# Attention and two feed-forward layers on one core: a shared block of tail keys, and fp32 value products in column halves of TensorE

## The chip, the cores and the metric

The kernel runs on one core of a Trainium2 chip. The metric is the device time of one execution in microseconds (us); lower is better. A difference of 0.2% (some 2.3 us here) is about the least that a measurement of this kernel tells from no change.

## The reference

Inputs are `q`, `k`, `v` of shape (4, 8, 576, 64) in fp32: 4 batches, 8 heads, 576 positions, 64 dimensions. Weights come in float64.

```python
q_rot, k_rot = (rotate(q), rotate(k))
scores = scale * np.matmul(q_rot, k_rot.transpose(0, 1, 3, 2))
scores = scores - np.max(scores, axis=-1, keepdims=True)
attn = np.exp(scores)
attn = attn / (np.sum(attn, axis=-1, keepdims=True) + 1e-09)
attn_out = np.matmul(attn, v).astype(np.float32)
x = attn_out.transpose(0, 2, 1, 3).reshape(B * S, H * D)   # 2304 x 512
h = x @ w_in;  g = h * np.clip(h + 3.0, 0.0, 6.0) / 6.0;  x = g @ w_out      # 512 -> 2048 -> 512
h = x @ w_in2; g = h / (1.0 + np.exp(-1.702 * h));        out = g @ w_out2
```

## The kernel before

A planner (`Plan`) collects operations with an engine, a duration, a sort key and their buffers; `run` simulates the engines with these durations and writes each engine's instructions in the order that it finds. The table `C` holds the keys' offsets and buffer counts (`PB`, `PTB`). So a change to an operation's cost or key reorders the program far from it.

**fp32 by pieces.** A fast product takes operands in the type fp32r, which keeps fewer bits. To reach fp32 accuracy, an operand is split into a high part (a copy in fp32r) and a low part (the difference): names that end in `h` and `l`. A product is then three fast products (`qh kh`, `ql kh`, `qh kl`). A plain fp32 product needs no split; on TensorE (PE) it is two matmul records in the trace.

**Attention** (`attention`, `pair`) goes by pairs of heads, 16 in all, 4 for each batch. For a pair:
- q and k are rotated (mostly on GpSimd, POOL), transposed on PE (L498, L511) and split. `vhl` is the split of the values `rawv`, 64 high and 64 low columns for each of the 10 blocks.
- Queries are blocks c = 0 to 3 of 128, and a block of the last 64 of either head (`P[8]`). `both` makes the scores of block c for both heads (L558): each head uses 64 rows of PE, so the two heads' products stand in the two row halves. `tail` makes those of the last queries (L545). VectorE (DVE) takes the maximum of each 576 keys (L531), ScalarE (ACT) the exponential (L533) into a buffer `P`.
- Values: for each head, the five key blocks j = 0 to 4 (the fifth has 64 keys) of `P` are transposed on PE, four transposes for a block (L611, 40 in a pair). ACT copies a block out of PSUM to `PTh` (L615), DVE takes the low part `PTl` (L632) or, for the tail block, puts it below the high part (L619). Then two products with `vhl` (L638), or one for the tail block (L623), give 128 rows: the part of the values' high columns and that of their low columns. In batches 0 and 1 some blocks j go as a plain fp32 product instead (L628): 64 columns of PE, `PTh` unsplit; the table's `F00` to `F21` say how many, 4 a pair in batch 0, 5 in batch 1, none in batches 2 and 3. ACT copies half of the bank to `otmp`, DVE adds (L645), and a product with the transposed reciprocal sums (L670, L678) finishes the pair.
- The last queries: `P[8]` is transposed (L580), split in `P8h` and `P8l`, and multiplied in nine products (L598); ACT and DVE join the two halves (L661, L663), and L672 transposes.

**The first layer** (`moe1`) runs batch by batch while the next batch's attention goes on, so its products (L814, L839) stand between the attention's; batch 0 has no layer beside it, only the weights' conversion (L719 to L728). The second layer (L1027 to L1139) follows when attention is done.

Of the kernel before, what the change touches and what calls it, by code (L numbers as in the profile page):

```python
# [30 lines left out]
C = {'T0': 59.504, 'D1': 12.604, 'LN1': 168.009, 'LN2': 130.306, 'LN3': 403.413, 'LM': 383.596, 'X': 32.498,  # L31
# [7 lines left out]
HOOK = None  # L39

# [40 lines left out]
class Plan:  # L81
# [70 lines left out]
    def run(self):  # L152
# [39 lines left out]
        def place(o):  # L192
# [16 lines left out]
            if at and sum(f) < 2 and nxt["PS"][0] not in o.news:  # L209
                return None  # L210
            return at

        def can(o):
# [6 lines left out]
            for t, k in need.items():  # L220
                room = self.caps[t] - used[t]
                if room < k:
                    return False
                if room <= k and any(b not in o.news for b in nxt[t][:k]):
                    return False
# [12 lines left out]
        total = len(self.ops)  # L238
        while done < total:
            moved = True  # L240
            while moved:
                moved = False
                for e in engines:
# [15 lines left out]
                    if e == "PE" and o.mode != mode:  # L259
                        for x in ready[e]:  # L260
                            if x.key[0] > o.key[0] + C["MODE"]:
                                break
                            if x.mode == mode and can(x):
                                o = x
                                break
                    for x in o.alts:
                        ready[x].remove(o)
                    o.ns, o.fn = o.alts[e]
                    for b, i in place(o):
# [10 lines left out]
                    if e == "PE":  # L280
                        if o.mode != mode:
                            o.ns += 95
                        mode = o.mode
# [11 lines left out]
                    for x in o.begun:  # L295
                        x.n -= 1
                        if x.n == 0:
                            x.taken = (now, o)
                            heapq.heappush(events, (max(now, x.t0), seq, "put", x))
                            seq += 1  # L300
            if not events:
# [43 lines left out]

def act(n, psum=False, acc=False):
    return (170 if psum else 205) + 0.833 * n + 200 * acc
# [19 lines left out]
def attention_moe_moe(ctx: ExitStack, tc: tile.TileContext, q, k, v, w_in, w_out, w_in2, w_out2,  # L367
# [49 lines left out]
    def full(b, n, h):  # L417

        return C[f"F{min(b, 2)}{h}"]

    def attention(apool, pp, gpool, wtile, tabs, xf_of, at):
# [5 lines left out]
        for i, (r, parts) in enumerate(((rq, ((64, 128, 0), (0, 64, 1))), (rk, ((64, 128, 0), (64, 128, 1))))):  # L427
            def zero(r=r, parts=parts):
                for lo, hi, h in parts:
                    nc.gpsimd.memset(r.t[lo:hi, h, 4, :], 0.0)  # L430
            plan.op("Pool", 200, -100 + i, zero, w=[(r, "z")])

        def pair(n):
# [19 lines left out]
            rv = Buf(plan, apool, "rawv", [128, 2, 5, D], F32, 2)  # L453
            sm = v[b, h0:h0 + 2, 0:512, :].rearrange("h (p r) d -> p h r d", r=4)
            tl = v[b, h0:h0 + 2, 512:576, :].rearrange("h p d -> p h d")
            kv = kd + 1.0
            plan.op("SP", 475, kv, lambda: nc.sync.dma_start(rv.t[:, :, 0:4, :], sm), w=[(rv, 0)], kb=256, after=[lq])
            plan.op("SP", 630, kv, lambda: nc.sync.dma_start(rv.t[0:64, :, 4, :], tl), w=[(rv, 1)], kb=64, after=[lq])
            plan.op("SP", 630, kv, lambda: nc.sync.dma_start(rv.t[64:128, :, 4, :], tl), w=[(rv, 2)], kb=64, after=[lq])
# [52 lines left out]
            kh = Buf(plan, apool, "kh", [128, S], F32R, 2)  # L512
            kl = Buf(plan, apool, "kl", [128, S], F32R, 2)
# [677 lines left out]
```

## Time and profile before

| | |
|---|---|
| time, median of 3 runs (lowest to highest) | 1135.84 us (1135.81 to 1136.01) |
| span of the profiled execution, first to last instruction | 1134.3 us, 1.5 us less than the median run |
| PE busy | 1098.7 us, 97% |
| DVE, ACT, POOL busy | 713.2, 558.9, 645.3 us |

No time of the profiled execution is given beside its span. PE is busy nearly all the time; how far its records overlap is read from the distance of their starts, since a record lasts longer than the distance to the next.

### The profile page before, as it was taken

How to read it: one execution, taken by the hardware profiler on the slowest of the kernel's cores; microseconds unless marked ns; L12 is line 12 of the kernel's file. 1: busy time of each engine (PE TensorE's matmuls, PEld its weight loads, DVE VectorE, ACT ScalarE, POOL GpSimd, SP SyncE). 2: the span in 40 equal slices, each digit the busy share in tenths (PEclk: the TensorE clock that was granted, in tenths of full speed). 3: DMA queues.
4: the chain of work that ended last, by engine and by line, in shares of the span. 5: the costliest groups of instructions: out<-in, count | busy, mean ns of one | idle time of the engine just before them, and what ended most of it. 6: DMA issues, size and time to landing. Idle time of an engine off the chain costs nothing.

```text
span 1134.3 us, 16742 instructions
## 1 busy us (share of the span) xinstructions
PE 1098.7 (97%) x6264; PEld 898.2 (79%) x6264; DVE 713.2 (63%) x1092; ACT 558.9 (49%) x1133; POOL 645.3 (57%) x640
## 2 busy tenths in 40 slices
PE   5999999999999999999999999999999999999995
PEld 4666777777888888878887888888888888888884
DVE  5788777877656665566664544655655655566543
ACT  5788766666755564655556412444323433333330
POOL 5875876969563477363326435466645647455440
PEclk9999999999999999999999999999999999999998
DMA  3434565656543545443337543122102011120012
GB/s 92 129 129 142 160 225 165 212 183 206 171 130 111 153 151 181 120 141 107 112 112 260 157 140 85 66 74 75 42 34 75 19 56 37 39 74 21 19 75 93
DMA packets 58888, 129.69 MB, mean 114 GB/s; under 512 B 13752, under 2 KB 26808, under 8 KB 58040
## 3 DMA queue, kind: packets, MB, share of 16 engines
q1 hardware_dynamic: 44712, 78.13, 21.4%
q0 software_dynamic: 13824, 50.34, 14.7%
q8 instruction: 49, 0.80, 0.3%
q14 instruction: 31, 0.25, 0.1%
q10 hardware_dynamic: 272, 0.16, 0.0%
HBM read 103.97 MB, written 24.64 MB: 113 GB/s over the span
## 4 chain that ended last, share of the span: by engine, by line
PE 92%; DVE 5%; ACT 1%; issue 0%; DMA 0%; SPq 0%; DVEq 0%; ACTq 0%
PE psum L839 17%; PE psum L1139 17%; PE psum L814 17%; PE psum L1027 11%; PE psum L1067 6%; PE psum L611 6%; PE psum L558 5%; PE psum L638 4%; PE psum L628 3%; PE psum L598 1%; PE psum L545 1%; DVE sc L531 1%; DVE cvt L728 1%; PE psum L498 1%; PE psum L580 1%; PE psum L623 1%
## 5 line engine op out<-in xcount | busy, mean ns | idle before, releaser
L391 POOL TENSOR_TENSOR gl<-t,gh 128x512 fp32r<-128x512 f32 (+1 forms) x144 | 184.4, 1284 | 138.0 <-ACT gh L401 118.9
L533 ACT ACTIVATE P<-psum,sc 128x576 f32<-128x576 f32 x144 | 105.5, 739 | 60.4 <-DVE sc L531 60.0
L531 DVE TENSOR_REDUCE sc<-psum 128x1 f32<-128x576 f32 x144 | 102.6, 752 | 35.4 <-PE psum L558 31.8
L1145 DVE TENSOR_TENSOR oacc<-oacc,psum 128x512 f32<-128x512 f32 x124 | 85.0, 686 | 48.9 <-PE psum L1139 47.4
L615 ACT ACTIVATE PTh<-psum 128x512 fp32r<-128x512 f32 (+2 forms) x160 | 89.0, 598 | 49.3 <-PE psum L611 48.0
L1139 PE MATMUL psum<-woh,gh 128*128 128x512 f32 x284 | 111.2, 392 | 0.0
L1139 PE MATMUL psum<-woh,gl 128*128 128x512 f32 x284 | 110.8, 390 | 0.0
L1139 PE MATMUL psum<-wol,gh 128*128 128x512 f32 x284 | 110.7, 390 | 0.0
L401 ACT ACTIVATE gh<-t 128x512 fp32r<-128x512 f32 (+1 forms) x134 | 81.1, 607 | 53.3 <-DVE t L1035 25.7
L814 PE MATMUL psum<-xh,wih 128*128 128x512 f32 x256 | 105.7, 413 | 1.5 <-DVE t L821 1.2
L839 PE MATMUL psum<-gh,woh 128*128 128x512 f32 x256 | 104.3, 407 | 0.1
L848 DVE TENSOR_TENSOR y<-y,psum 128x512 f32<-128x512 f32 x112 | 76.4, 685 | 42.5 <-PE psum L839 41.7
L814 PE MATMUL psum<-xh,wil 128*128 128x512 f32 x256 | 100.5, 393 | 0.0
L839 PE MATMUL psum<-gh,wol 128*128 128x512 f32 x256 | 100.4, 392 | 0.0
L814 PE MATMUL psum<-xl,wih 128*128 128x512 f32 x256 | 100.3, 392 | 0.0
L839 PE MATMUL psum<-gl,woh 128*128 128x512 f32 x256 | 100.2, 391 | 0.0
L821 DVE SCALAR_TENSOR_TENSOR t<-t,psum 128x512 f32<-128x512 f32 (+1 forms) x80 | 50.0, 631 | 68.2 <-ACT t L819 68.0
L611 PE MATMUL psum<-ident,P 128*128 128x128 f32 (+1 forms) x640 | 87.9, 275 | 2.7 <-ACT P L533 1.2
L611 PEld LDWEIGHTS psum<-ident,P 128*128 128x128 f32 (+1 forms) x640 | 71.6, 135 | 23.6 <-issue 4.7
L819 ACT ACTIVATE t<-psum,three 128x512 f32<-128x512 f32 (+1 forms) x80 | 50.7, 644 | 79.8 <-PE psum L814 62.4
L1035 DVE TENSOR_TENSOR t<-t,psum 128x512 f32<-128x512 f32 (+1 forms) x52 | 31.5, 606 | 78.3 <-ACT t L1033 68.1
L632 DVE TENSOR_TENSOR PTl<-psum,PTh 128x512 fp32r<-128x512 f32 x92 | 61.5, 685 | 29.0 <-ACT PTh L615 28.7
(193 smaller groups left out, 2936.7 us busy)
## 6 DMA issues: line engine op xcount, KB each, us to landing
raw<-in_moe_w_in_dram SPq DMA_DIRECT2D x32, 512.0 KB, 3.8
raw<-in_moe_w_out_dram SPq DMA_DIRECT2D x32, 512.0 KB, 3.6
wih<-w_hl POOLq DMA_DIRECT2D x24, 512.0 KB, 4.4
wil<-w_hl POOLq DMA_DIRECT2D x24, 512.0 KB, 5.2
woh<-w_hl POOLq DMA_DIRECT2D x24, 512.0 KB, 4.4
wol<-w_hl POOLq DMA_DIRECT2D x24, 512.0 KB, 5.0
rawq<-in_q_dram SPq DMA_DIRECT2D x16, 256.0 KB, 3.0
rawk<-in_k_dram SPq DMA_DIRECT2D x16, 256.0 KB, 2.8
```

The source lines that it names most:

```text
L391: alts = [("Pool", ns or gps(n), lambda: nc.gpsimd.tensor_tensor(o(), i0(), i1(), op=op)), ("DVE", dve(n), lambda: nc.vector.tensor_tensor ...
L401: alts = {"ACT": ("ACT", act(n, psum), lambda: nc.scalar.activation(o(), i(), AF.Copy, scale=scale)), "DVE": ("DVE", dve(n, not psum), lam ...
L531: plan.op("DVE", dve(S), key + C["oM"], lambda: nc.vector.tensor_reduce(sc.t[:, i:i + 1], Sp.t[:, :, :HS], axis=AX.XY, op=ALU.max, negate= ...
L533: plan.op("ACT", act(S, True, True), key + C["oE"], lambda: nc.scalar.activation(halves(P[i].t), Sp.t[:, :, :HS], AF.Exp, bias=sc.t[:, i:i ...
L611: nc.tensor.transpose(T.t[:m, 0, c * 128:c * 128 + 128], P[hs + c].t[:, j * 128:j * 128 + m], ident)
L615: plan.op("ACT", act(512, True), key + C["oTh"], lambda T=T, hi=hi, m=m, fp=fp: nc.scalar.activation(hi.t.bitcast(F32) if fp else hi.t[:m] ...
L814: nc.tensor.matmul(hp.t[:, 0, :n], ww.t[:, cc, fs], xx.t[:, cc, :n], start=(cc == 0 and i == 0), stop=(cc == CC - 1 and i == 2))
L839: nc.tensor.matmul(yp.t[:, 0, :n], ww.t[:, a, cs], xx.t[:, a, :n], start=(i == 0), stop=(i == 3 * G - 1))
L848: plan.op("DVE", dve(n), ka + C["oY"], lambda yp=yp, y=y, c=c, n=n: nc.vector.tensor_tensor(y.t[:, c, :n], y.t[:, c, :n], yp.t[:, 0, :n], ...
L1027: nc.tensor.matmul(hp.t[:, 0, :n], ww.t[:, cc, fs], xx.t[:, cc, :n], start=(cc == 0 and i == 0), stop=(cc == CC - 1 and i == 2))
L1139: nc.tensor.matmul(op_.t[:, 0], xx.t[:, ts], ww.t[:, a, :], start=(i == 0), stop=(i == 3 * G - 1))
L1145: plan.op("DVE", dve(512), key, lambda op_=op_, tt=tt: nc.vector.tensor_tensor(oacc.t[:, tt], oacc.t[:, tt], op_.t[:, 0], op=ALU.add), r=[ ...
```

## The change

All batches take one path now (`FP` lists all five blocks for each batch).
- The tail keys: `kh` and `kl` get 64 more columns in front, into which POOL copies the 64 tail keys. The second head's scores run over tail, then main keys, so that in the pair's joint buffer `P[c]` (1152 columns) the two heads' tails stand side by side. One transposed block of 128 keys serves both heads: 36 transposes for a pair. `rawv` holds the two heads' tail values in a block that is zero elsewhere (POOL clears it once).
- The values: no split. One fp32 product of the shared tail block over all 128 columns of PE, then for each j = 0 to 3 head 0's product into columns 0 to 63 and head 1's into columns 64 to 127, all in one bank and in one run. ACT copies the bank to `xf`; `otmp`, the addition, `vhl`, `PTl` and DVE's part in them are gone.
- The last queries: five fp32 products of 128 columns instead of nine split ones of 256.
- The planner's rules for banks and buffers, its costs for a change of PE's mode, and the table `C` are changed too.

```diff
+FP = ((0, 1, 2, 3, 4), (0, 1, 2, 3, 4), (0, 1, 2, 3, 4), (0, 1, 2, 3, 4))
...
+            for x in range(2):
+                plan.op("SP", 550, kv, lambda x=x: nc.sync.dma_start(
+                    rv.t[64 * x:64 * x + 64, 8 + x, :], v[b, h0 + x, 512:576, :]), w=[(rv, 1 + x)], kb=32, after=[lq])
...
+            for kk in (kh, kl):
+                plan.op("Pool", gps(64, True), key, lambda kk=kk: nc.gpsimd.tensor_scalar(
+                    kk.t[:, :64], kk.t[:, S:].bitcast(F32), 1.0, 1.0, op0=ALU.mult, op1=ALU.mult), r=[(kk, "m")], w=[(kk, "t")])
...
-                P[c], P[4 + c] = [Buf(plan, pp, "P", [128, S], F32, C["PB"]) for _ in range(2)]
+                P[c] = Buf(plan, pp, "P", [128, 2 * S], F32, C["PB"])
...
-                                                 kk.t[xs, hf * HS:(hf + 1) * HS], start=i == 0, stop=i == 2)
+                                                 kk.t[xs, 64 * (1 - x) + hf * HS:64 * (1 - x) + (hf + 1) * HS], start=i == 0, stop=i == 2)
...
+                    nc.tensor.matmul(E.t[:, 0, 128:256].rearrange("p (h d) -> p h d", h=2), h8.t[:, j * 128:j * 128 + 128],
+                                     rv.t[:, 0:8].rearrange("p (h j) d -> p h j d", h=2)[:, :, j] if j < 4 else rv.t[:, 8:10],
+                                     start=(j == 0), stop=(j == 4))
...
+                    off = 128 * j if j == 4 or h == 0 else S + 64 + 128 * j
...
+                            nc.tensor.transpose(T.t[:, 0, c * 128:c * 128 + 128], P[c].t[:, off:off + 128], ident)
...
+                        if j == 4 and allfp:
+                            nc.tensor.matmul(Os[0].t[:, 0], flat(rv.t[:, 8:10]), parts[4, 0][0].t.bitcast(F32), start=j == js[0], stop=False)
...
+                    for j in js:
+                        if j in fp and j < 4:
+                            for h in range(2):
+                                nc.tensor.matmul(Os[h].t[hrow(h), 0], rv.t[:, 4 * h + j], parts[j, h][0].t.bitcast(F32), start=False, stop=allfp and j == 3)
...
+            if allfp:
+                copy(key, 512, lambda: xf.t[:, hp, :512], lambda: Os[0].t[:, 0], [Os[0]], [(xf, h0), (xf, h0 + 1)], also=("ACT", "DVE"), psum=True)
```

How the order moves is shown at three places. The first is PE in batch 0, where the second pair's values are made. Before (transposes L611, a fast product L623, fp32 products L628):

```order
L611 MATMUL psum<-ident,P 128x128 x4
L628 MATMUL psum<-PTh,rawv 64x512
L611 MATMUL psum<-ident,P 128x128 x4
L628 MATMUL psum<-PTh,rawv 64x512
L611 MATMUL psum<-ident,P 128x128 x4
L611 MATMUL psum<-ident,P 64x128 x4
L623 MATMUL psum<-PTh,vhl 128x512
```

Now (L569 last queries' scores, L615 their products, L650 the tail block, L664 the column halves, L700 a transpose, L582 the next pair's scores):

```order
L569 MATMUL psum<-kl,qh 128x288
L615 MATMUL psum<-rawv,P8h 128x128 x5
L650 MATMUL psum<-PT,rawv 128x512
L664 MATMUL psum<-PT,rawv 64x512 x8
L700 MATMUL psum<-ident,t_622 128x128
L582 MATMUL psum<-kh,qh 128x288 x2
```

The fp32 products, one at a time between transposes before, stand in one run of eight behind the tail block. The second place is ACT, over the copies of a pair's transposed blocks in batch 0. Before (L615 the copies, L533 exponentials, L401 other copies, L515 `kh`):

```order
L515 ACTIVATE kh<-psum 128x576
L615 ACTIVATE PTh<-psum 128x512 x2
L401 ACTIVATE vhl<-rawv 128x10x64
L615 ACTIVATE PTh<-psum 128x512 x2
L401 ACTIVATE xh<-xf 128x512
L615 ACTIVATE PTh<-psum 64x512
L533 ACTIVATE P,sc<-psum,sc 128x576 x2
```

Now (L632 the copies, L557 exponentials, L535 `kh`, L424 other copies):

```order
L557 ACTIVATE P,sc<-psum,sc 128x576 x4
L535 ACTIVATE kh<-psum 128x576
L424 ACTIVATE P8h<-psum 128x512
L632 ACTIVATE PT<-psum 128x512 x9
L424 ACTIVATE P8h<-psum 64x128 x2
L557 ACTIVATE P,sc<-psum,sc 128x576 x2
```

All nine copies stand together, behind the pair's last exponentials and ahead of the next pair's first. The third place is PE in the last batch, where the first layer's products (L839; now L842) stand around a pair's values. Before:

```order
L598 MATMUL psum<-vhl,P8h 128x256
L638 MATMUL psum<-PTh,vhl 128x512
L638 MATMUL psum<-PTl,vhl 128x512
L839 MATMUL psum<-gh,woh 128x512
L839 MATMUL psum<-gl,woh 128x512
```

Now:

```order
L842 MATMUL psum<-xl,wih 128x512
L842 MATMUL psum<-xh,wil 128x512
L650 MATMUL psum<-PT,rawv 128x512
L664 MATMUL psum<-PT,rawv 64x512 x8
L582 MATMUL psum<-kh,qh 128x288 x2
```

The split products, spread in twos between the layer's, became one run here as well.

## Rows read from the trace of the kernel before

**Rows 1.** The page: busy time by engine, and the chain that ended last.

```profile
PE 1098.7 (97%) x6264; PEld 898.2 (79%) x6264; DVE 713.2 (63%) x1092; ACT 558.9 (49%) x1133; POOL 645.3 (57%) x640
...
PE 92%; DVE 5%; ACT 1%; issue 0%; DMA 0%; SPq 0%; DVEq 0%; ACTq 0%
```

**Rows 2.** Windows: stretch, length, then busy us of PE, PEld, DVE, ACT, POOL.

```profile
20.00:140.00 120.00, 111.70 (x733) 79.09 (x734) 96.73 (x144) 97.80 (x220) 92.33 (x84) 1.00 0.41 131
140.00:300.00 160.00, 159.29 (x896) 118.55 (x895) 119.95 (x179) 105.73 (x218) 123.09 (x113) 1.00 0.64 202
300.00:550.00 250.00, 250.00 (x1476) 204.23 (x1474) 157.01 (x245) 140.57 (x291) 133.81 (x146) 1.00 0.45 134
550.00:620.00 70.00, 67.76 (x389) 55.74 (x386) 45.24 (x69) 38.97 (x81) 27.49 (x31) 1.00 0.52 174
```

**Rows 3.** Chain that ended last, 40 to 75 us: start, us, what.

```profile
53.12 0.69 DVE PTh L619
...
53.86 0.73 PE psum L638 x2
```

**Rows 4.** Timeline of PE: start, us, line, out<-in, count, idle before.

```profile
32.47 1.93 PE L628 MATMUL psum<-PTh,rawv 128*64 128x512 f32 x4
...
47.23 0.71 PE L511 MATMUL psum<-ident,roped 128*128 128x128 f32 x5
47.77 1.91 PE L611 MATMUL psum<-ident,P 128*128 128x128 f32 x16
...
60.55 0.47 PE L623 MATMUL psum<-PTh,vhl 128*128 128x512 f32 x1
60.95 0.40 PE L558 MATMUL psum<-kh,qh 64*128 64x288 f32 x2
61.19 0.29 PE L558 MATMUL psum<-kh,ql 64*128 64x288 f32 x2
61.32 0.29 PE L558 MATMUL psum<-kl,qh 64*128 64x288 f32 x2
...
61.94 0.50 PE L638 MATMUL psum<-PTh,vhl 128*128 128x512 f32 x1
62.28 0.40 PE L638 MATMUL psum<-PTl,vhl 128*128 128x512 f32 x1
62.61 1.07 PE L628 MATMUL psum<-PTh,rawv 128*64 128x512 f32 x2
63.61 0.66 PE L580 MATMUL psum<-ident,P 128*128 128x128 f32 x4
...
64.68 0.40 PE L638 MATMUL psum<-PTh,vhl 128*128 128x512 f32 x1
64.92 0.39 PE L638 MATMUL psum<-PTl,vhl 128*128 128x512 f32 x1
...
67.24 0.28 PE L598 MATMUL psum<-vhl,P8h 128*128 128x256 f32 x1
67.36 0.29 PE L598 MATMUL psum<-vhl,P8l 128*128 128x256 f32 x1
...
69.74 0.71 PE L511 MATMUL psum<-ident,roped 128*128 128x128 f32 x5
```

**Rows 5.** Line L628: weight loads and records, ns minimum/median/maximum.

```profile
L628 PEld LDWEIGHTS psum<-PTh,rawv x72: 132/136/137, 29.5 to 273.3; 128*64 128x64 f32 x72
L628 PE MATMUL psum<-PTh,rawv x72: 592/592/644, 29.5 to 273.7; 128*64 128x512 f32 x72
```

**Rows 6.** Timeline of ACT: exponentials, then copies of transposed blocks.

```profile
24.52 0.73 ACT L533 ACTIVATE P<-psum,sc 128x576 f32<-128x576 f32 x1
...
25.24 0.74 ACT L533 ACTIVATE P<-psum,sc 128x576 f32<-128x576 f32 x1
...
25.96 2.07 ACT L615 ACTIVATE PTh<-psum 128x512 fp32r<-128x512 f32 x4
```

**Rows 7.** POOL groups by form: count, busy, mean ns, idle before.

```profile
L391 POOL TENSOR_TENSOR t<-rawk,tab 128x640 f32<-128x640 f32 x30 | 48.7, 1643 | 0.5
```

More of the change, by code (lines that the diff above doesn't have):

```diff
@@ L208, in place, with head @@
                 at.append((b, c[0]))
-            if at and sum(f) < 2 and nxt["PS"][0] not in o.news:
+            if at and sum(f) < 2 and not loose and head() not in o.news:
                 return None
             return at
+        def head():
+            for b in nxt["PS"]:
+                if all(x.tag == "PS" or used[x.tag] < self.caps[x.tag] for x in b.first.news):
+                    return b
         def can(o):
@@ L223, in can @@
                     return False
-                if room <= k and any(b not in o.news for b in nxt[t][:k]):
+                if (room <= k or t in STRICT) and any(b not in o.news for b in nxt[t][:k]):
                     return False
@@ L262, in run @@
                                 break
-                            if x.mode == mode and can(x):
+                            if not switch(mode, x.mode) and can(x):
                                 o = x
                                 break
+                    got = place(o)
+                    loose = False
                     for x in o.alts:
@@ L268, in run @@
                     o.ns, o.fn = o.alts[e]
[L269 removed]
+                    for b, i in got:
                         b.b0 = i
@@ L300, in run @@
                             seq += 1
+            if not events and not loose:
+                loose = True
+                if VERBOSE:
+                    print('loose', now)
+                continue
             if not events:
@@ L594, in pv8 @@
+            for x in range(2):
+                copy(key + C["oTh"], 128, lambda x=x: h8.t[64 * x:64 * x + 64, 512:], lambda: E.t[:64, 0, :128], [(E, 0)], [(h8, 1 + x)],
+                     also=("ACT", "DVE"), psum=True)
             def pv8():
                 for j in range(5):
-                    rh = vhl.t.rearrange("p (h j) a d -> p h j (a d)", h=2)[:, :, j]
-                    for i, x in enumerate((h8, l8) if j < 4 else (h8,)):
-                        nc.tensor.matmul(E.t[:, 0, 128:384].rearrange("p (h x) -> p h x", h=2), x.t[:, j * 128:j * 128 + 128], rh,
-                                         start=(j == 0 and i == 0), stop=(j == 4))
@@ L607, in pair, with tp @@
+            Os = [Banks(plan, 1)] * 2 if allfp else [Banks(plan, 1) for _ in range(2)]
+            parts = {}
+            for j in range(5):
+                for h in range(2) if j < 4 else (0,):
+                    key = f(C["TT"] + C["TS"] * (2 * j + h if j < 4 else -1 if allfp else 8))
                     T = Banks(plan, 1)
-                    def tp(T=T, j=j, m=m, hs=hs):
+                    off = 128 * j if j == 4 or h == 0 else S + 64 + 128 * j
+                    def tp(T=T, off=off):
@@ new lines, in pair @@
+                    hi = Buf(plan, pp, "PT", [128, 512], F32R, C["PTB"])
+                    if j in fp:
+                        plan.op("ACT", act(512, True), key + C["oTh"], lambda T=T, hi=hi: nc.scalar.activation(
+                            hi.t.bitcast(F32), T.t[:, 0], AF.Copy), r=[T], w=[hi],
+                            alts=[("DVE", dve(512), lambda T=T, hi=hi: nc.vector.tensor_copy(hi.t.bitcast(F32), T.t[:, 0]))])
+                        parts[j, h] = (hi, None)
+                        continue
@@ L632, in pair @@
+                    lo = Buf(plan, pp, "PT", [128, 512], F32R, C["PTB"])
+                    plan.op("ACT", act(512, True), key + C["oTh"], lambda T=T, hi=hi: nc.scalar.activation(
+                        hi.t, T.t[:, 0], AF.Copy), r=[T], w=[hi, lo])
                     plan.op("DVE", dve(512), key + C["oTl"], lambda T=T, hi=hi, lo=lo: nc.vector.tensor_tensor(
                         lo.t, T.t[:, 0], hi.t.bitcast(F32), op=ALU.subtract), r=[T, hi], w=[lo])
[L635 to L638 removed]
@@ L639, in pair @@
[L639 to L647 removed]
+                    parts[j, h] = (hi, lo)
@@ new lines, in pair @@
+            key = f(C["PV"] + C["TS"] * 9.5)
+            if allfp:
+                copy(key, 512, lambda: xf.t[:, hp, :512], lambda: Os[0].t[:, 0], [Os[0]], [(xf, h0), (xf, h0 + 1)], also=("ACT", "DVE"), psum=True)
+            else:
+                tmp = Buf(plan, pp, "otmp", [128, 512], F32, 1)
+                for h in range(2):
+                    copy(key, 512, lambda h=h: tmp.t[hrow(h)], lambda h=h: Os[h].t[hrow(1 - h), 0], [Os[h]], [(tmp, h)], also=("ACT", "DVE"), psum=True)
+                    plan.op("DVE", dve(512), key, lambda h=h: nc.vector.tensor_tensor(
+                        xf.t[hrow(h), hp, :512], Os[h].t[hrow(h), 0], tmp.t[hrow(h)], op=ALU.add),
+                        r=[Os[h], (tmp, h)], w=[(xf, h0 + h)])
```

161 lines of the change are left out of this document (68 added, 93 removed), and 14 rows, old and new, of the table C.

## Prediction

> **What bounds the kernel now.** I read the page first: PE is busy 97% of the span and the chain that ended last is 92% PE [rows 1]. Then the windows, since an average hides stages. From 300 to 550 us PE has no idle time at all, from 140 to 300 us 0.7 us; only from 20 to 140 us, where batch 0's attention has no layer beside it, is it idle 8.3 us of 120, with DVE and ACT at 81% each [rows 2]. Another 2.2 us are lost from 550 to 620, where attention ends. So nearly everywhere the time is the sum of PE's own work, and relief of DVE, ACT and POOL is worth something only in batch 0. There the chain runs through DVE too: a tail block's low part, 0.69 us, ends just ahead of the two products that use it [rows 3]. That stage goes by pairs: the transposes of k (L511) start at 47.23 and 69.74, so a pair takes 22.51 us [rows 4].
>
> Busy time can't price PE's work, as records overlap; I take distances of starts [rows 4]. Twenty-one transposes against five: 16 in 1.91 us and 5 in 0.71, so 1.20 for 11, **0.109** each. A fast product of 512 columns: 64.68 to 64.92 and the next, **0.23**. One of 256: 67.24 to 67.36, **0.12**. An fp32 record in 64 columns: four take 1.93 us, the last runs 0.592 [rows 5], so (1.93 - 0.592) / 3 = **0.446**, two records a product. Two row halves together: 61.19 to 61.32, **0.13** for both. That equals what one such product would need alone, so two halves of PE do work at once in this kernel; it is shown for row halves of fast products only.
>
> **The change part by part.**
>
> *Transposes.* 36 a pair for 40: 64 x 0.109 = **-7.0 us**.
>
> *Value products.* Before, 216 fast products (8 x 4 x 2 less those in fp32, and the tail blocks: 92 x 2 + 32) x 0.23 = 49.7, and 36 fp32 products x 2 x 0.446 = 32.1; together 81.8. Now, a pair: the tail block over 128 columns, two records of 512 columns, 0.89 (the row is for 64 columns; the number of moving columns is the same). Then eight products in column halves. Nothing in the trace shows two column halves at once. If each had to wait for the other: 16 x 0.446 = 7.14. If all overlapped: 8 x 0.446 = 3.57. The order issues head 0's two records ahead of head 1's two; if records start in order and a half takes one at a time, head 1 runs one record behind and the run takes 9 x 0.446 = 4.01. I take 4.01: the row halves overlap fully, which is the nearest row, and in the single fp32 products the weight loads of 0.136 already hide behind the records (0.446 is the whole distance) [rows 4, 5]. 16 x (0.89 + 4.01) = 78.4: **-3.4 us**. By batches: it costs 0.8 us a pair where there were no fp32 products (batches 2 and 3) and gives back 0.9 and 1.4 in batches 0 and 1. Bounds: -10.5 to +46.7.
>
> The Trainium skill, "TensorE: Matmul & The Clock Gate", section "What overlaps and what doesn't", says that weight loads overlap running matmuls only where their rows of the array differ. Two column halves share all rows, so by that rule 16 loads of 0.136 a pair would lie open, 35 us in all; the single column half above, whose loads hide, does not agree with it.
>
> *Last queries.* 144 records x 0.12 = 17.3 before; now five fp32 products with 128 moving columns, ten records a pair. None of that shape is in the trace; nearest is the fp32 transpose, 128 columns, 0.109: 17.4, **+0.1**. Were it 0.23, +19.
>
> *Changes of PE's division.* Products in a column half cost time at both ends: 61.94 to 62.61 is 0.67 for two fast products (0.46 elsewhere), and 62.61 to 63.61 is 1.00 for 0.89 [rows 4]. That is 0.32; only the exit's 0.11 is seen everywhere; I take 0.25. The order has 30 such stretches before and 16 now: 14 x 0.25 = **-3.5** (bounds -1.5, -4.5). Row-half stretches go from 62 to 57; entry and exit of one cost 0.17 and 0.2 (60.55 to 60.95 for 0.23, then 0.99 to 61.94 for 6 x 0.13). Against these five stand a dozen more alternations of transposes with the layer's products; I take both together as nothing.
>
> *Other engines.* DVE loses 92 low parts, 32 tail parts, 32 additions and more, ACT the copies to `otmp` and `vhl`, POOL a few splits. Past 140 us these are hidden by PE, so nothing is gained. POOL gets two copies of 64 columns a pair, on which the second head's scores wait; behind it in POOL's queue stand rotations. They follow `kh` and `kl` while PE does 36 transposes, 3.9 us: no cost. If POOL is in the middle of a rotation, 1.64 us [rows 7], still none; if that cover were gone, at most some 2 us a pair in batch 0, +8. SP issues as many transfers as before, two of them of half the size.
>
> *Waits in batch 0.* PE's work in one of its pairs before: 60 transposes 6.5, scores 24 x 0.13 + 6 x 0.13 = 3.9, four fp32 products 3.6, ten fast ones 2.3, nine of 256 columns 1.1, changes of division about 2.2: 19.6. The pair took 22.5, so 2.9 was waiting. Now: 56 transposes 6.1, scores 3.9, values 4.9, last queries 1.1, changes 1.1: 17.1. Will PE wait as much? An exponential follows the one before at 25.24 - 24.52 = 0.72; copies follow at (2.07 - 0.6) / 3 = 0.49 [rows 6]; DVE's maxima keep the exponentials' pace. From the last exponential of a pair at 0: PE transposes until 3.9, ACT's nine copies end at 5.2 behind them; scores of block 0 and of the last queries, their product, the tail block and the column halves fill PE until 12.5 and need three exponentials, long done. Then the scores of blocks 1, 2, 3 come at once, six exponentials with little on PE between: block 2 waits about 1.1 us for PSUM, and the next 36 transposes about 1.2 us for the last exponential, at 19.4. So 2.3 of waiting for 2.9: 0.6 x 4 pairs, and little else: **-2.0**. Bounds: all 8.3 us of idle time gone, or the 22.5 us a pair kept, which gives 2.5 x 4 = 10 us of the sum back.
>
> **Sum.** -7.0 - 3.4 + 0.1 - 3.5 - 2.0 = -15.8. From the median of 1135.8 (the span of 1134.3 and 1.5 around it) that is **1120.0 us**.
>
> **Rivals.**
> 1. *Column halves do not overlap, slower than before.* Place: the run of eight. Price: 7.14 for 4.01, 3.13 x 16 = +50: 1170. It decides from a run longer than 4.01 + 15.8 / 16 = 5.0 us, an overlap factor under 7.14 / 5.0 = 1.43. For it: no row shows column halves at once. Both streams need all 128 rows, which row halves don't. Against it: row halves overlap wholly, and an fp32 record takes 0.446 for what a fast one does in 0.23, so each stream asks for columns at half the pace.
> 2. *They overlap in part.* With a factor of 1.6 the run takes 7.14 / 1.6 = 4.46, +0.45 x 16 = +7: 1127. The Trainium skill, same page, "Measured speedup vs the span model", gives 2.38 for three column tiles, which is 1.59 for two in proportion; no run here shows it.
> 3. *Batch 0 keeps its 22.5 us a pair*, because the exponentials of three blocks stand in a row: +10 for what PE saves there and the 2.0: 1130.
> 4. *Batch 0's waits vanish.* DVE loses the low parts that ended PE's waits [rows 3], and the planner fills the gaps: -6 more, 1114.
>
> **How the numbers follow.** The forecast, 1116 to 1124, 0.57. Rival 1: 0.08; rival 2: 0.13; rival 3: 0.07; rival 4 (1108 to 1116): 0.15. Rival 1 is the slower side, with half of that beyond 1160. The range leaves it out and the edge of rival 4: **1110 to 1130**. Faster 0.89, within 0.2% (2.3 us, the least that a measurement of this kernel tells from no change) 0.03, slower 0.08.
>
> **What would show it.** In the profile after: the column halves' run from L664's first start to the next line's, 4.0 to 4.2 us (1: 7; 2: 4.5); last queries' records 0.11 apart; the distance of k's transposes in batch 0, 19 to 20 us; PE idle between 20 and 140 us, 5 to 8 us; none from 150 to 550. DVE's busy time falls by more than 100 us with no gain past 140 us. The prediction is wrong if the run is over 5 us, if new waits appear on PE beside the first layer (values now need all nine copies at once), or if the second head's scores wait for POOL.

## The result, and the profile after

| | before | after |
|---|---|---|
| time, median (lowest to highest) | 1135.82 us (1135.80 to 1136.01) | 1120.44 us (1120.09 to 1120.67) |
| ratio, 95% interval | | 0.9864 (0.9850 to 0.9878) |
| span of the profiled execution | 1134.3 us | 1118.1 us |

The gain is 15.4 us of median and 16.2 us of span. The page of the changed kernel, as in [rows 1]:

```profile
PE 1076.9 (96%) x6216; PEld 870.8 (78%) x6216; DVE 588.4 (53%) x877; ACT 538.8 (48%) x1104; POOL 636.6 (57%) x668
...
PE 88%; ACT 3%; POOL 3%; DVE 2%; DMA 2%; issue 1%; SPq 0%; DVEq 0%; POOLq 0%; ACTq 0%
```

DVE is busy 125 us less, and PE's share of the chain fell from 92% to 88%: PE waits more than before. The windows tell where. These are the stretches of [rows 2]; behind the five engines' busy times stand the granted clock of TensorE, the DMA share and GB/s:

```profile
20.00:140.00 120.00, 107.29 (x744) 77.99 (x746) 70.19 (x99) 97.87 (x223) 90.45 (x95) 0.97 0.45 149
140.00:300.00 160.00, 156.04 (x925) 117.93 (x922) 92.92 (x131) 104.18 (x219) 119.67 (x118) 1.00 0.58 190
300.00:550.00 250.00, 250.00 (x1465) 191.44 (x1465) 102.78 (x152) 129.54 (x275) 130.97 (x154) 1.00 0.45 137
550.00:620.00 70.00, 68.86 (x392) 56.60 (x392) 33.17 (x47) 39.72 (x83) 31.20 (x35) 1.00 0.55 184
```

PE's idle time in these stretches is 12.7, 4.0, 0 and 1.1 us; in [rows 2] it was 8.3, 0.7, 0 and 2.2. That is 6.6 us more, 4.4 of it in batch 0. Over the whole span PE's busy time fell by 21.8 us and its idle time (the span less the busy time) rose by 5.6 us, from 35.6 to 41.2. The next view is PE's timeline in batch 0 (start, us, line, idle time before and its releaser):

```profile
24.44 0.74 PE L531 MATMUL psum<-ident,roped 128*128 128x128 f32 x5 [1.06 <-ACT P L557]
...
45.48 0.77 PE L531 MATMUL psum<-ident,roped 128*128 128x128 f32 x5 [0.34 <-ACT P L557]
...
53.79 1.28 PE L615 MATMUL psum<-rawv,P8h 128*128 128x128 f32 x10
54.90 1.02 PE L650 MATMUL psum<-PT,rawv 128*128 128x512 f32 x2
55.86 3.65 PE L664 MATMUL psum<-PT,rawv 128*64 128x512 f32 x16
59.44 0.33 PE L700 MATMUL psum<-ident,t 128*128 128x128 f32 x1
...
62.90 0.40 PE L582 MATMUL psum<-kh,qh 64*128 64x288 f32 x2 [1.56 <-ACT P L557]
...
66.47 0.77 PE L531 MATMUL psum<-ident,roped 128*128 128x128 f32 x5
...
85.53 0.40 PE L582 MATMUL psum<-kh,qh 64*128 64x288 f32 x2 [2.46 <-ACT P L557]
...
89.61 0.77 PE L531 MATMUL psum<-ident,roped 128*128 128x128 f32 x5
```

Four things are read here. The run of column halves lasts 59.44 - 55.86 = 3.58 us. Inside it the records start in twos, as these cuts of the same timeline show:

```profile
56.34 0.60 PE L664 MATMUL psum<-PT,rawv 128*64 128x512 f32 x2
56.77 0.60 PE L664 MATMUL psum<-PT,rawv 128*64 128x512 f32 x2
```

The second two start 0.48 us behind the first, each further two 0.43 behind the ones before, and the next line 0.53 behind the last. So the 16 records need eight steps, and the two halves work at once with nothing lost. A single column half has the same steps in the kernel before (cuts of the first row of [rows 4]):

```profile
32.95 0.59 PE L628 MATMUL psum<-PTh,rawv 128*64 128x512 f32 x1
33.38 0.59 PE L628 MATMUL psum<-PTh,rawv 128*64 128x512 f32 x1
```

The prediction's 0.446 is thus the mean of one step of 0.48 and two of 0.43; by the starts a run of n steps takes n x 0.43 and 0.15 for its first step and its end. The last queries' ten records take 54.90 - 53.79 = 1.11, 0.11 each. The transposes of k stand 21.04, 20.99 and 23.14 us apart. And PE waits 1.56 and 2.46 us in the middle of a pair's scores (L582) for an exponential (L557) that frees their bank in PSUM.

### The profile page after: what moved, and what is told of

Read it like the earlier page. It is cut to its first block, busy times and chain, and to the rows that moved or that the text cites. A ratio compares the mean times of both kernels' runs of the same rounds, so it can differ in the third digit from the quotient of the medians.

```text
span 1118.1 us, 16407 instructions
## 1 busy us (share of the span) xinstructions
PE 1076.9 (96%) x6216; PEld 870.8 (78%) x6216; DVE 588.4 (53%) x877; ACT 538.8 (48%) x1104; POOL 636.6 (57%) x668
## 4 chain that ended last, share of the span: by engine, by line
PE 88%; ACT 3%; POOL 3%; DVE 2%; DMA 2%; issue 1%; SPq 0%; DVEq 0%; POOLq 0%; ACTq 0%
PE psum L1167 17%; PE psum L842 17%; PE psum L867 17%; PE psum L1055 11%; PE psum L1095 6%; PE psum L582 5%; PE psum L664 4%; PE psum L628 4%; PE psum L615 1%; ACT P L557 1%; PE psum L650 1%; PE psum L569 1%; POOL t L414 1%; PE psum L518 1%; PE psum L698 1%
## 5 line engine op out<-in xcount | busy, mean ns | idle before, releaser
L555 DVE TENSOR_REDUCE sc<-psum 128x1 f32<-128x576 f32 x144 | 102.4, 751 | 96.7 <-PE psum L582 81.4
L557 ACT ACTIVATE P<-psum,sc 128x576 f32<-128x576 f32 x144 | 105.6, 739 | 61.2 <-DVE sc L555 60.3
L842 PE MATMUL psum<-xh,wih 128*128 128x512 f32 x256 | 109.2, 426 | 0.0
L424 ACT ACTIVATE gh<-t 128x512 fp32r<-128x512 f32 (+1 forms) x134 | 81.0, 605 | 44.6 <-DVE t L1063 24.7
L842 PE MATMUL psum<-xh,wil 128*128 128x512 f32 x256 | 100.3, 392 | 0.0
L842 PE MATMUL psum<-xl,wih 128*128 128x512 f32 x256 | 100.3, 392 | 0.0
L849 DVE SCALAR_TENSOR_TENSOR t<-t,psum 128x512 f32<-128x512 f32 (+1 forms) x80 | 50.2, 632 | 94.8 <-ACT t L847 94.8
L632 ACT ACTIVATE PT<-psum 128x512 f32<-128x512 f32 x144 | 79.7, 611 | 37.7 <-PE psum L628 37.6
L628 PE MATMUL psum<-ident,P 128*128 128x128 f32 x576 | 77.9, 273 | 3.0 <-ACT P L557 1.6
L628 PEld LDWEIGHTS psum<-ident,P 128*128 128x128 f32 x576 | 66.9, 141 | 14.5 <-ACT P L557 2.4
L1055 PE MATMUL psum<-yh,wih 128*128 128x512 f32 (+1 forms) x208 | 74.9, 360 | 0.0
```

Source lines behind the costliest of these rows:

```text
L424: alts = {"ACT": ("ACT", act(n, psum), lambda: nc.scalar.activation(o(), i(), AF.Copy, scale=scale)), "DVE": ("DVE", dve(n, not psum), lam ...
L555: plan.op("DVE", dve(S), key + C["oM"], lambda: nc.vector.tensor_reduce(sc.t[:, i:i + 1], Sp.t[:, :, :HS], axis=AX.XY, op=ALU.max, negate= ...
L557: plan.op("ACT", act(S, True, True), key + C["oE"], lambda: nc.scalar.activation(halves(to()), Sp.t[:, :, :HS], AF.Exp, bias=sc.t[:, i:i + ...
L628: nc.tensor.transpose(T.t[:, 0, c * 128:c * 128 + 128], P[c].t[:, off:off + 128], ident)
L632: plan.op("ACT", act(512, True), key + C["oTh"], lambda T=T, hi=hi: nc.scalar.activation(hi.t.bitcast(F32), T.t[:, 0], AF.Copy), r=[T], w= ...
L842: nc.tensor.matmul(hp.t[:, 0, :n], ww.t[:, cc, fs], xx.t[:, cc, :n], start=(cc == 0 and i == 0), stop=(cc == CC - 1 and i == 2))
```

## The experiments

**1. Do column halves overlap, and what sets the run?** The second head's products behind all of the first's:

```diff
-                    for j in js:
-                        if j in fp and j < 4:
-                            for h in range(2):
+                    for h in range(2):
+                        for j in js:
+                            if j in fp and j < 4:
```

> The changed kernel, with the run of eight column-half products in another order: head 0's four blocks, then head 1's four, instead of the heads by turns; nothing else moves. In the profile of the changed kernel the run takes 3.58 us, 8 x 0.447, and its records start in twos. Theory A, PE starts records in the order of the program and a half takes one at a time: now eight records of one half stand ahead of the other half's, so nothing overlaps, the run takes 16 x 0.446 = 7.1 us, and the time is 1120.4 + 16 x 3.55 = 1177 us, a little less where batch 0 waits anyhow. Theory B, PE fetches records of the free half from behind, or a half's record is short by itself: run 3.6 us, time 1120 us.

1145.21 us, ratio 1.0080 (1.006 to 1.010). PE's timeline, first of the run's beginning alone, then of the whole run; behind it windows of its three thirds (records of L664 in brackets; one that runs over a boundary counts on both sides):

```profile
57.55 1.93 PE L664 MATMUL psum<-PT,rawv 128*64 128x512 f32 x4
...
57.55 5.42 PE L664 MATMUL psum<-PT,rawv 128*64 128x512 f32 x16
62.90 0.33 PE L700 MATMUL psum<-ident,t 128*128 128x128 f32 x1
```

```profile
57.50:59.30 1.80, 1.75 (x4) 0.60 (x5) 1.00 0.00 0
59.30:61.10 1.80, 1.80 (x10) 0.73 (x9) 1.00 0.00 0
61.10:62.90 1.80, 1.80 (x6) 0.40 (x3) 1.00 0.00 0
```

The run is 62.90 - 57.55 = 5.35 us, not the expected value of either theory. It is 12 steps (12 x 0.43 + 0.15 = 5.31): four records of head 0 stand alone (1.93 us for four, as for single products in [rows 4]), then records come in twos, and at the end four of head 1 stand alone. The profile doesn't name a record's half, but strict order would need 15 steps. So a record for the free half starts ahead of records that still wait for the other half, but only some four places ahead: the ninth record starts with the fifth. In the kernel's own order, two records of each head by turns, the free half always finds one within reach. 1.77 us more in 16 runs would be 28.3 us; 24.8 was measured.

The same question from the other side: of j = 0 to 2, head 1's products go into the first half too and are added to head 0's, so that only the last product of head 1 is alone in its half.

```diff
-                                nc.tensor.matmul(Os[h].t[hrow(h), 0], rv.t[:, 4 * h + j], parts[j, h][0].t.bitcast(F32), start=False, stop=allfp and j == 3)
+                                nc.tensor.matmul(Os[h].t[hrow(h if j == 3 else 0), 0], rv.t[:, 4 * h + j], parts[j, h][0].t.bitcast(F32), start=False, stop=allfp and j == 3)
```

> The changed kernel, but for j = 0 to 2 both heads' products go into columns 0 to 63 (head 1's values are then added to head 0's, so the output is not the reference's); only j = 3 still has one head in each half. Order and number of instructions stay. If the short run comes from the two halves working at once, 12 records stand one after the other and 4 in twos: (12 + 2) x 0.446 = 6.2 us a run, +2.67 x 16 = +43, 1163 us. If a record of the fp32 product is simply short here (0.22 us), nothing changes: 1120 us.

1158.10 us, ratio 1.0193 (1.0173 to 1.0214).

```profile
57.42 6.22 PE L664 MATMUL psum<-PT,rawv 128*64 128x512 f32 x16
63.57 0.33 PE L700 MATMUL psum<-ident,t 128*128 128x128 f32 x1
```

```profile
61.76 1.08 PE L664 MATMUL psum<-PT,rawv 128*64 128x512 f32 x4
```

The run is 6.15 us, the 14 steps (14 x 0.43 + 0.15 = 6.17) that 14 records in one half and two beside them ask for. The first two that start together do so at 61.76, ten steps into the run: the fifteenth record starts with the eleventh, again four places ahead. The number of records and of weight loads is the same as in the changed kernel; only the place of the columns differs. That the halves work at once is shown, and is worth 37.7 us here.

**2. What is PE's own work worth?** The four transposes of the shared tail block are done twice.

```diff
-                        for c in range(4):
+                        for c in range(4) if off != 512 else (0, 1, 2, 3, 0, 1, 2, 3):
```

> The changed kernel with the four transposes of the shared tail block done twice into the same bank: four more transposes a pair, as many as the kernel before had, and nothing else. If PE's work is what counts everywhere, 64 x 0.109 = +7.0 us: 1127.4. If batch 0's waits swallow it there, 12 pairs count: +5.2, 1125.7. If the order hides it altogether, 1120.4.

1127.06 us, ratio 0.9917 (0.9901 to 0.9934): 6.6 us over the changed kernel, for 64 transposes of 0.109 (7.0 us). Four transposes a pair are what the shared block saves, so the first term of the prediction's sum holds.

**3. The value products of the late batches.** Batches 2 and 3 go back to split values and fast products, on the new shared tail block.

```diff
-FP = ((0, 1, 2, 3, 4), (0, 1, 2, 3, 4), (0, 1, 2, 3, 4), (0, 1, 2, 3, 4))
+FP = ((0, 1, 2, 3, 4), (0, 1, 2, 3, 4), (), ())
```

> The changed kernel with plain fp32 products in batches 0 and 1 only; in batches 2 and 3 the main blocks go as split fast products again (with the shared tail block, whose products stand in row halves). By the prediction's prices fp32 costs 4.9 us a pair there and the split 18 x 0.23 = 4.1, so this is 8 x 0.8 = 6 us faster: 1114 us. By the runs of 3.58 and 0.95 us that the profile after shows, fp32 costs 4.5 us and the split 16 x 0.23 = 3.7 and 0.5 to 0.9 for the tail in row halves with its entry and exit: even, 1118 to 1122 us. Rival: the DVE work that comes back (some 9 x 0.7 us a pair) makes PE wait beside the first layer: over 1124 us.

1132.51 us, ratio 0.9972 (0.9961 to 0.9984), 12.1 us over the changed kernel. Windows of this run:

```profile
140.00:300.00 160.00, 152.96 (x896) 117.67 (x893) 98.98 (x138) 101.59 (x213) 116.36 (x117) 0.99 0.57 187
300.00:550.00 250.00, 246.10 (x1446) 198.64 (x1445) 153.50 (x220) 136.34 (x287) 134.04 (x154) 1.00 0.45 135
```

PE is idle 3.9 us between 300 and 550, where the changed kernel has none, and 7.0 from 140 to 300 (4.0). PE's busy time in all is 1080.9 us, 4.0 more than in the changed kernel. So this run costs mostly by waits, and doesn't price the two kinds of product against each other; that stays open. Its time lies in the rival's range, and 2.5 of the 3.9 us end with DVE (L679 and L849); but its order was not fitted to it either, and no run parts the two causes.

**4. How much of the gain hangs on the order?** The changed program with the table `C` of before (but its own buffer counts, `PB` 5 and `PTB` 12):

> The changed kernel with the table of offsets (C) of the kernel before, all but the two buffer counts PB and PTB, which fit the new buffers. The work on PE is the same, only the order differs. If the sum of PE's work makes the gain, most of it stays, and the differences are waits in batch 0 and stretches: 1120 to 1128 us. If the gain lies in the new order that the table makes, it is 1128 us or more.

1137.79 us, ratio 1.0013 (1.0004 to 1.0023). The whole gain is gone, though PE's busy time, 1081.5 us, is nearly that of the changed kernel. Its windows and two of PE's waits (us, times, longest):

```profile
20.00:140.00 120.00, 101.12 (x705) 73.89 (x706) 67.62 (x90) 90.72 (x208) 86.62 (x90) 0.97 0.43 138
140.00:300.00 160.00, 151.81 (x891) 116.21 (x888) 99.67 (x135) 102.12 (x217) 118.26 (x117) 0.97 0.59 190
```

```profile
PE psum L582 <- ACT P L557: 10.1, 13, 2.2
...
PE psum L604 <- ACT P L557: 6.7, 2, 4.5
```

PE is idle 18.9 and 8.2 us in the two stretches. And the other way, the program of before with the new table (its own buffer counts):

> The kernel before with the changed kernel's table of offsets (all but the counts PB and PTB); no other change. If the new table is better by itself, it carries part of the gain: 1120 to 1132 us. If a table fits only the program it was made for, waits appear as in the changed kernel with the old table: over 1138 us.

1170.49 us, ratio 1.0302 (1.0287 to 1.0318). Of these two, each table fits only its own program. The new table is no gain by itself; without it the change is none.

**5. What makes PE wait in batch 0?** First, every second copy of a transposed block in batch 0 goes to DVE, which has time there:

```diff
-                        plan.op("ACT", act(512, True), key + C["oTh"], lambda T=T, hi=hi: nc.scalar.activation(
+                        plan.op("ACT", act(512, True), key + C["oTh"], (lambda T=T, hi=hi: nc.vector.tensor_copy(
+                            hi.t.bitcast(F32), T.t[:, 0])) if b == 0 and (2 * j + h) % 2 else lambda T=T, hi=hi: nc.scalar.activation(
```

> The changed kernel, but in batch 0 every second copy of a transposed block (four of a pair's nine) is done by DVE where it was done by ACT; PE's order is unchanged. In the profile of the changed kernel PE waits 9.3 us in nine waits for an exponential before the scores of block 2 or 3, and little for copies. Theory 1, these waits come from three blocks' scores in a row, whose six exponentials pace PE: the copies lie elsewhere, so 1119 to 1121 us. Theory 2, ACT's whole load in a pair sets the pace of batch 0: four copies at 0.5 us less on ACT is 2 us a pair, 6 to 8 us in all, 1113 us.

1120.89 us, ratio 0.9864 (0.9849 to 0.9879): nothing, and the waits of L582 stay (9.6 us). ACT's copies don't set the pace. Next, the run of column halves of the first three pairs is cut: the second half waits until the next pair's block 1 has its scores, so that PE has work between them (the edit makes `pair` a generator):

```diff
+            both(1, f(0.4))
+            yield steps[-1]
...
-            for js in PVS[allfp]:
+            for js in ((4, 0, 1), (2, 3)) if n < NPAIR - 1 else PVS[allfp]:
+                wait = []
+                if js == (2, 3):
+                    wait = [(yield)]
```

> The changed kernel, but for the first three pairs the run of column halves is cut in two (tail block and j = 0, 1; then j = 2, 3), and the second run is held back until the next pair's scores of block 1 are issued, so that it lies between the scores of block 1 and of block 2. It adds three entries and exits of column halves, about 0.3 us each. Theory 1 (PE waits between blocks 1 and 2 because six exponentials follow one another): 1.8 us of work fills waits of 1.6 to 2.5 us in three pairs, and the stretch of half clock behind two of them goes too: -4 to -6 us, 1114 to 1116. Theory 2 (ACT's load sets batch 0's pace): the wait only moves to the transposes, 1120 to 1122 us.

1130.13 us, ratio 0.9942 (0.9927 to 0.9957), 9.7 us slower than the changed kernel, which neither theory had. The waits of L582 fell only from 9.3 to 7.1 us, others came, and the pairs in batch 0 became 23.8, 23.6 and 26.6 us long. PE was idle 16.2 us from 20 to 140 us, and the granted clock there was 0.93 (12.7 us and 0.97 in the changed kernel). That the later values held up what follows them is likely but not shown.

So the releaser itself was looked at. Ahead of the first of these waits, at 41.90 us, stand on DVE, on ACT and on PE of the changed kernel:

```profile
38.64 1.67 DVE L756 SCALAR_TENSOR_TENSOR cvt<-raw,cvt 128x512 int32<-128x512 int32 x1
40.23 1.41 DVE L555 TENSOR_REDUCE sc<-psum 128x1 f32<-128x576 f32 x2
```

```profile
40.34 0.63 ACT L424 ACTIVATE wih<-cvt 128x512 fp32r<-128x512 f32 x1 [0.99 <-DVE cvt L756]
41.01 0.74 ACT L557 ACTIVATE P<-psum,sc 128x576 f32<-128x576 f32 x1
```

```profile
41.90 0.60 PE L582 MATMUL psum<-kh,qh 64*128 64x288 f32 x2 [1.68 <-ACT P L557]
42.30 0.44 PE L582 MATMUL psum<-kh,ql 64*128 64x288 f32 x2
42.54 0.44 PE L582 MATMUL psum<-kl,qh 64*128 64x288 f32 x2
```

A step of the weights' conversion (L756) holds DVE, then the maxima (L555), then ACT's split of a weight block, then the exponential. Behind the wait the scores stand 0.24 us apart instead of 0.13: TensorE runs at the lower of its two levels, 1.2 GHz. Such a stretch stands behind the wait of 2.46 us too, none behind that of 1.56. The granted clock by windows:

```profile
40.00:42.20 2.20, 0.52 (x4) 0.31 (x4) 2.20 (x4) 1.82 (x4) 1.84 (x2) 0.94 0.96 250
42.20:44.90 2.70, 2.70 (x24) 2.59 (x22) 1.13 (x3) 1.76 (x5) 2.62 (x4) 0.50 0.76 284
86.40:89.60 3.20, 2.86 (x21) 2.52 (x18) 2.90 (x6) 2.31 (x6) 1.28 (x1) 0.50 0.44 161
```

The test shortens the two conversion steps on DVE and keeps every engine's order:

```diff
-                    t.t.bitcast(I32), t.t.bitcast(I32), 3, raw.t[:, :, 0], op0=ALU.logical_shift_left, op1=ALU.bitwise_or),
+                    t.t[:, :64].bitcast(I32), t.t[:, :64].bitcast(I32), 3, raw.t[:, :64, 0], op0=ALU.logical_shift_left, op1=ALU.bitwise_or),
...
-                    t.t.bitcast(I32), raw.t[:, :, 1], -2 ** 31, t.t.bitcast(I32), op0=ALU.bitwise_and, op1=ALU.bitwise_or),
+                    t.t[:, :64].bitcast(I32), raw.t[:, :64, 1], -2 ** 31, t.t[:, :64].bitcast(I32), op0=ALU.bitwise_and, op1=ALU.bitwise_or),
```

> The changed kernel, in its own order, but VectorE's two steps of the weights' conversion (L753, L756) work on 64 of the 512 columns of each piece; the other 448 are left out. In batch 0 the longest waits of PE stand behind such steps: at 38.64 us an L756 of 1.67 us is ahead of two maxima (L555) that a block's exponentials need, and PE waits until 41.90. Theory 1 (the maxima are late, because conversions stand ahead of them on VectorE): PE's idle time from 20 to 140 us falls from 12.7 to 8 us or less, the half clock behind the waits goes too: 1112 to 1116. Theory 2 (ScalarE's own row of exponentials and copies sets these waits, whatever VectorE does): idle time stays above 11 us, 1119 to 1120.5.

1117.24 us, ratio 0.9832 (0.9816 to 0.9848): 3.2 us under the changed kernel, between the two theories. The first line of its page, its window of batch 0, and PE's waits over one pair:

```profile
PE 1073.8 (96%) x6216; PEld 867.8 (78%) x6216; DVE 526.3 (47%) x877; ACT 537.3 (48%) x1104; POOL 617.9 (55%) x668
```

```profile
20.00:140.00 120.00, 108.47 (x762) 77.39 (x760) 57.16 (x100) 99.17 (x225) 89.67 (x97) 1.00 0.49 157
```

```profile
41.20 0.40 PE L582 MATMUL psum<-kh,qh 64*128 64x288 f32 x2 [1.13 <-ACT P L557]
...
44.05 0.76 PE L531 MATMUL psum<-ident,roped 128*128 128x128 f32 x5 [0.98 <-ACT P L557]
46.22 4.30 PE L628 MATMUL psum<-ident,P 128*128 128x128 f32 x36 [0.68 <-ACT P L557]
...
61.12 0.40 PE L582 MATMUL psum<-kh,qh 64*128 64x288 f32 x2 [1.24 <-ACT P L557]
```

The clock is 1.00 in the whole stretch (0.97 before this edit), and the longest wait of L582 fell from 2.5 to 1.3 us, but idle time only from 12.7 to 11.5. Over the span PE's busy time fell by 3.1 us, with the same 6216 records, and its idle time rose by 0.6. So over the whole span what this run gained was the lower clock, not the waits themselves. What is left is a regular pattern in each pair: some 1.2 us at the scores and 1.0 and 0.7 at the transposes, all for exponentials.

The run with the heads apart (experiment 1) shows that the long waits hang on where a step falls. Its conversion is whole, but its longest wait of L582 is 1.3 us: ahead of the first pair's wait of 1.13 us the step is done before the scores are, and holds up no maximum.

```profile
38.38 1.64 DVE L756 SCALAR_TENSOR_TENSOR cvt<-raw,cvt 128x512 int32<-128x512 int32 x1
41.17 1.43 DVE L555 TENSOR_REDUCE sc<-psum 128x1 f32<-128x576 f32 x2 [1.15 <-PE psum L582]
```

The last of these tests takes ACT's part by itself, in the kernel's order (the sums that it leaves out are replaced by 1, so batch 0 is not normalized):

```diff
                     halves(to()), Sp.t[:, :, :HS], AF.Exp, bias=sc.t[:, i:i + 1], scale=1.0,
-                    accum_out=sc.t[:, 9 + i:10 + i]), r=[Sp, (sc, i)], w=[P[8] if i == 8 else (P[i % 4], i // 4), (sc, 9 + i)])
+                    **({} if b == 0 else dict(accum_out=sc.t[:, 9 + i:10 + i]))), r=[Sp, (sc, i)], w=[P[8] if i == 8 else (P[i % 4], i // 4), (sc, 9 + i)])
```

> The changed kernel, in its own order, but batch 0's exponentials don't sum their rows, and POOL sets the reciprocals' input to 1: the normalization of batch 0 is left out. An exponential with its sum follows the one before at 0.72 us, of which the reading of the sum is 0.09. Theory 1 (the maxima on VectorE are what is late): nothing, 1119.5 to 1121. Theory 2 (ScalarE's row of six exponentials sets the pace of a pair in batch 0): 6 x 0.09 a pair, 2 us in all: 1117.5 to 1118.5.

1119.90 us, ratio 0.9857 (0.9842 to 0.9872): not told from the changed kernel. The exponentials follow one another only 0.05 us sooner than before (0.67 for 0.72), which by theory 2 is 6 x 0.05 x 4 = 1.2 us, less than a measurement of this kernel tells. Idle time did fall, from 12.7 to 11.2 us. So this run doesn't decide between the theories. Whether the maxima on DVE that feed them set this pace was not tried alone.

**6. Do POOL's copies of the tail keys cost?** First with the copies planned twice (`for kk in (kh, kl, kh, kl)`):

> The changed kernel, but POOL copies the 64 tail keys of kh and kl twice: two copies more for each pair. Theory of the prediction (the copies are hidden, since scores come after the transposes): 1120.4, and PE's waits on POOL as they were. Rival (second heads' scores wait for POOL): some 0.5 us for each pair, 1126 to 1130.

1133.64 us, ratio 0.9976 (0.9965 to 0.9986), 13.2 us slower. But PE waits nowhere for the copies, and the planner had written another order: in the first pair, the products L650 and L664 went ahead of the next pair's scores. So the copies were doubled again, now inside one planned operation, which leaves every queue in the changed kernel's order:

```diff
-                plan.op("Pool", gps(64, True), key, lambda kk=kk: nc.gpsimd.tensor_scalar(
-                    kk.t[:, :64], kk.t[:, S:].bitcast(F32), 1.0, 1.0, op0=ALU.mult, op1=ALU.mult), r=[(kk, "m")], w=[(kk, "t")])
+                plan.op("Pool", gps(64, True), key, lambda kk=kk: [nc.gpsimd.tensor_scalar(
+                    kk.t[:, :64], kk.t[:, S:].bitcast(F32), 1.0, 1.0, op0=ALU.mult, op1=ALU.mult) for x in range(2)][1], r=[(kk, "m")], w=[(kk, "t")])
```

> The changed kernel with each of POOL's copies of the tail keys done twice, one instruction behind the other inside the same planned operation, so that every engine keeps the changed kernel's order and POOL alone gets 32 instructions of 0.24 us more. Theory 1 (the copies are hidden; the time of the run with two more planned copies for each pair, 1133.6, was its other order): 1120 to 1121.5. Theory 2 (the copies lie on the path of the second head's scores): 2 x 0.24 us a pair, 8 us in all: 1126 to 1130, with waits of PE on POOL's kh and kl.

1121.98 us, ratio 0.9876 (0.9860 to 0.9893): 1.5 us over the changed kernel, nearer to theory 1 and less than a measurement of this kernel tells. One wait of PE for a copy appears, in batch 0:

```profile
74.59 0.40 PE L582 MATMUL psum<-kl,qh 64*128 64x288 f32 x1 [0.63 <-POOL kl L539]
```

Idle time from 20 to 140 us is 14.7 us (12.7 without the edit); past batch 0 it has not grown, and from 300 to 550 us there is none. So if the second copies, in the same order, cost anything, it is in batch 0 alone, and the single ones are hidden elsewhere. The other 12 us of the first attempt came with its other order.

## Why the prediction was right, and which steps failed

The forecast was 1120.0 us, the time is 1120.4; that they agree so closely is luck. The sum had 13.8 us less work on PE and 2.0 us less waiting. PE's busy time fell by 21.8 us, and its idle time rose by 5.6. These are errors of 8.0 and 7.6 us in opposite directions.

- **Transposes, -7.0: right.** Doing the saved ones again costs 6.6.
- **Value products, -3.4: the mechanism was right, the size was not.** The halves do work at once. But the run of eight was taken as 9 x 0.446 = 4.01, because records were thought to start in order; it measured 3.58: -0.43 x 16 = -6.9 us more. Head 1 runs no record behind, so there is no ninth step. The step itself is 0.43, not 0.446; that the measured run looks like 8 x 0.446 is chance, as its first step and its end add 0.15. The row halves of before, which were the nearest row, gave the right factor of 2. The Trainium skill, "TensorE: Matmul & The Clock Gate", section "The mechanism", under "What overlaps and what doesn't", says that a weight load overlaps running matmuls only where their rows differ, which would have laid open the 16 weight loads of a run. The trace doesn't agree with that: no time is left for them in 3.58 us.
- **Last queries, +0.1: right** (0.11 a record, where 0.109 was taken).
- **Changes of division, -3.5, and more alternations, 0: not tested by themselves.** One reading behind the 0.25 is off: of the 0.21 at a stretch's entry, 0.11 stands in the first product behind the scores (61.94 to 62.28 [rows 4]), not at the column half. What the trace gives is a count by distances of starts over the whole span, idle time left out, which charges a change to the record ahead of it. By it the value products took 91.2 us before and 73.1 now: -18.1, where this term and the one above had -6.9. The first layer's same 1920 products went from 410.9 to 415.1 us: 4.2 more, where the alternations were put at nothing without a row.
- **Other engines, 0: right from 300 to 550 us.** There PE has no idle time before or after, so DVE's 125 us less could bring nothing. From 140 to 300 us new waits of 3.3 us stand against it. POOL's copies are hidden past batch 0 (experiment 6).
- **Waits in batch 0, -2.0: this step failed, in sign too.** Idle time from 20 to 140 us rose by 4.4 us (12.7 for 8.3), and over the span by 5.6. The first fault is in the 2.9 us a pair that PE was said to wait before. They were what the priced work left of 22.5 us, not a reading. Windows over that pair before, and over three pairs after:

```profile
47.23:69.74 22.51, 20.86 (x142) 14.19 (x142) 18.96 (x30) 18.92 (x44) 16.99 (x16) 1.00 0.40 134
```

```profile
24.44:45.48 21.04, 18.51 (x134) 13.40 (x134) 12.21 (x16) 16.41 (x39) 19.22 (x20) 0.92 0.40 119
45.48:66.47 20.99, 17.76 (x138) 12.56 (x139) 14.05 (x20) 18.05 (x44) 17.81 (x18) 1.00 0.47 145
66.47:89.61 23.14, 19.46 (x139) 14.01 (x139) 12.92 (x20) 18.48 (x43) 15.04 (x17) 0.93 0.52 174
```

PE waited 22.51 - 20.86 = 1.65 us in the pair before. (Four times 2.9 is 11.6, more than the 8.3 us of idle time in [rows 2].) So the 2.3 us that the walk found meant some 0.65 more a pair, not 0.6 less. The second fault is smaller: PE waits 2.5, 3.2 and 3.7 us in the pairs after, not 2.3. "DVE's maxima keep the exponentials' pace" left out the weights' conversion, which shares DVE and ACT with the maxima and exponentials. With the conversion short, the waits are 2.6, 2.9 and 3.1 us, in the pattern that the walk named: 1.1 before block 2's scores (1.13 to 1.28 measured) and 1.2 before the transposes (0.98, with 0.68 behind it). The walk also left out the lower clock, which is in PE's busy time, some 3 us (experiment 5). So the distance of k's transposes is 21 to 23 us and not the predicted 19.4; with the short conversion it is 19.7, 20.6 and 21.4.

**The rivals.** The first (no overlap) and the second (factor 1.6) are refuted by the run of 3.58 us and the run in one half. The third, that batch 0 keeps its 22.5 us a pair, came true for the greater part (21.7 us a pair), by the mechanism that it names with the conversion on top of it; its total of 1130 did not come, because the value products paid for it. The fourth, no waits at all, is refuted.

**Of the signs that were named:** last queries and DVE's busy time came as told. The run came shorter, and PE's idle time from 20 to 140 us came above the 5 to 8 us. From 140 to 300 us PE is idle 4.0 us where it was idle 0.7, beside the first layer: that is one of the three signs by which the prediction called itself wrong, and its account of the waits is, though its total held. What the prediction didn't have among its rivals at all is the order: the same instructions by the old table take 1137.8 us.

## What to carry to other kernels

A total that comes out right proves no step: two errors of some 8 us hid each other here, and only steps measured apart (one run's length, one stage's idle time) told them. Where a planner writes the order, an edit's price is known only with the order held still: two small copies a pair cost 13 us with the order that they brought about, and without it 1.5, which is within the noise. A wait that is taken as what priced work leaves carries the errors of all prices; the idle time of the same stretch can be read. And a walk by hand through a stage has to take in everything that its engines do there, including work for a later stage.

## What the runs showed of the hardware

- Plain fp32 products in the two column halves of PE overlap fully: 16 records start in twos 0.43 us apart and take 3.58 us, and a single half has the same step of 0.43. A record for the free half starts ahead of waiting ones, from four places behind: with eight records of one head ahead of eight of the other, the run takes 12 steps, and with 14 of one half ahead of two, 14. What sets the reach is open.
- Behind an idle time of 1.68 us, with other gaps ahead of it, the granted clock was 0.50 for 2.7 us, and score records stood 0.24 instead of 0.13 us apart. It was 0.50 behind a wait of 2.46 us too, and 1.00 behind one of 1.56. With the waits of L582 at 1.3 us and less it stayed at 1.00 throughout batch 0 in the run with the short conversion; but in the run with the heads apart, where they are as short, it was 0.50 behind waits of 1.13, 0.98 and 0.68:

```profile
47.90:51.30 3.40, 3.40 (x16) 3.40 (x17) 1.36 (x2) 2.71 (x5) 3.31 (x3) 0.50 0.28 105
```

So the longest wait alone does not tell whether the clock falls.
